# A fused attention, gated MLP and expert-routing kernel: a hand-written order for its first part, and one PSUM operand in the VectorE instructions of the routing

## The chip, the cores and the metric

The kernel is one launch on one core of a Trainium2 chip. The metric is the device time of that launch in microseconds (us), the median of several runs. Engines are named as in the profile: PE (TensorE), DVE (VectorE), ACT (ScalarE), POOL (GpSimd), and SP, whose queue issues nearly all the DMAs.

## What is computed

Three layers follow one another. B, H, S, DH are 8, 8, 576, 64; N is 4608 tokens, D 512, F 1024, E 8 experts, 576 tokens for each.

```python
scores = q @ k.T / 8 * Dmat              # Dmat[i,j] = gamma_h ** (i-j) for i >= j, else 0
x = (scores @ v)                         # heads side by side: [4608, 512]
y = ((x @ w1) * (x @ w2)) @ w3 @ w_out   # weights in float64, [512,1024] [1024,1024] [1024,512]
logits = y @ w_gate                      # [4608, 8]
# greedy: all logits in falling order; a token takes its expert if it has none yet
# and the expert has fewer than 576 tokens
out[token] = relu(y[token] @ ew1[e]) @ ew2[e]
```

## The kernel before

**Attention** goes by 36 tiles of 128 tokens (two chunks of 64). The decay is split into a factor on q and one on k: `att_scale` (L257, DVE for the first ten tiles), `att_T` transposes both on PE and copies them out on ACT, `att_QK`, `att_mask` (DVE), `att_P` (the k-v product of each chunk), `att_state` (DVE adds it to the running state), `att_AV`, and `att_out`: a copy by ACT, an add on DVE, then the result as a high part (ACT) and a low part (POOL, L345). Three tiles make one block of 384 tokens in `XT`.

**MLP.** `ab(i)` (L534) works a block: for each of 8 slices `f` it makes `x @ w1` and then `x @ w2`. Each of these is one **pass**: 12 matmuls of 128x384 (L549), three for each of 4 row blocks, since x and the weights are split into a high and a low part. After the first pass of a slice ACT copies the PSUM bank out (L556), after the second DVE multiplies (L558). The weights come as 64-bit floats in pieces of 256 columns (`load_pair`, 1 MB each); `conv` (L184) makes one unit of 128 columns from them with an absolute value on ACT (L196), four DVE instructions (L197 to L202), a copy on ACT (L215) and one more DVE instruction (L216). `ab(0)` needs all 16 units of w1 and w2; `LEAD` says how far ahead of a slice they are converted. w3 is multiplied by w_out beforehand (`w34_all`), whose first PE instructions are the transposes of L391.

**Order.** The generators above are interleaved by `merge` (L66), which takes from a side generator whatever the main one's declared cost pays for. That gives priorities; a list scheduler then orders each engine's instructions by its own estimate of when they are ready. In `begin` (L1093) attention tiles, conversions and `ab(0)`, `ab(1)` are merged so. `ORDER` (L23) is the order of the first loads on SP's queue: q, k, v of tiles 0 to 2, pieces w0 to w3 of the weights, three pieces c of the constants.

**Routing** (`route`, L787) finds one threshold per expert in five rounds. `propose` (L691) masks the logits that fail, takes the best expert of each token (`best`, L666) and moves the result to experts' rows (`LP`). `search` (L706) then takes 6 steps: two counts on DVE (L716, L717) and one on ACT (L719), a matmul that adds them up over partitions (L676), and three to four very short DVE instructions (L726, L728, L729, L725) that move the thresholds. `place` (L746) turns the result into the list of row numbers by comparisons with a ramp `iota` on DVE (L774) beside products on POOL (L773), and 48 matmuls (L779). All along, `merge` interleaves the 24 late output tiles (`y_late`, L875): each has 24 matmuls (L893), a high part by ACT (L888) and a low part by POOL (L889, 128x1024).

The eight experts follow (`expert`, L997), in a block whose order comes from the scheduler.

## Time and profile before

| | |
|---|---|
| median of 3 runs | 1333.74 us (1332.22 to 1334.24) |
| the profiled execution's own time | 1332.78 us |
| its span, first to last instruction | 1330.8 us |
| mean granted PE clock | 0.976 of full |
| PE busy | 1261.4 us (95%) |
| DVE busy | 573.7 us (43%) |
| ACT busy | 460.2 us (35%) |
| POOL busy | 262.7 us (20%) |

PE is busy nearly throughout, so the table says little by itself. Idle time of PE stands in three places: the first 140 us, the routing from about 710 to 886 us, and the end. The other engines matter where PE waits for them.

### The profile page before, as it was taken

The page shows a single profiled execution, that of the slowest core. Times are in us where ns is not written, and L with a number is a line of the kernel's source. Part 1 is how long each engine was busy: PE and PEld are TensorE (multiplying, and loading weights), DVE is VectorE, ACT ScalarE, POOL GpSimd, SP SyncE. Part 2 cuts the span into 40 slices and gives each one's busy share as a digit, 9 for nine tenths or more (in the row PEclk, how much of TensorE's full clock was granted, in tenths as well). Part 3 has the DMA queues.
Part 4 walks back from the last instruction along what each step waited for, and adds up shares of the span by engine and source line. Part 5 has one row for each costly group of instructions (what it writes and reads, how often), then busy time and mean ns, then how long its engine had stood idle before and what let it go on. Part 6 is the DMA issues. An engine that isn't in the chain of part 4 may idle for free. (4 is left out here: it accounts for less than half of the span.)

```text
span 1330.8 us, 27168 instructions
## 1 busy us (share of the span) xinstructions
PE 1261.4 (95%) x11406; PEld 1114.0 (84%) x11406; DVE 573.7 (43%) x1298; ACT 460.2 (35%) x987; POOL 262.7 (20%) x238
## 2 busy tenths in 40 slices
PE   5789999999999999999999899869999999999996
PEld 4688988889898998988997676669989989899885
DVE  6796544443232222212215777564524435335220
ACT  4443333343223222222222434234534435335321
POOL 0101111112112020211013533261211202201011
PEclk7799999999999999999999999879999999999999
DMA  8756444422313122242014112044524425334110
GB/s 229 231 168 183 128 136 137 118 75 55 81 23 87 35 66 77 68 127 81 10 48 163 52 40 87 34 155 135 170 69 138 146 84 159 113 118 151 40 45 28
DMA packets 156382, 136.00 MB, mean 102 GB/s; under 512 B 119264, under 2 KB 119520, under 8 KB 155232
## 3 DMA queue, kind: packets, MB, share of 16 engines
q1 hardware_dynamic: 150368, 115.35, 29.4%
q0 software_dynamic: 5888, 18.88, 4.3%
q8 instruction: 91, 1.49, 0.4%
q14 instruction: 35, 0.29, 0.1%
HBM read 107.19 MB, written 27.00 MB: 101 GB/s over the span
## 5 line engine op out<-in xcount | busy, mean ns | idle before, releaser
L549 PE MATMUL p<-x,ws 128*128 128x384 f32 x2304 | 424.1, 339 | 3.1 <-issue 1.6
L549 PEld LDWEIGHTS p<-x,ws 128*128 128x128 f32 x2304 | 398.2, 189 | 11.2 <-issue 4.7
L1032 PE MATMUL p<-ws,g 128*128 128x512 f32 x864 | 218.1, 394 | 1.9 <-DVE rs L1042 1.4
L1032 PEld LDWEIGHTS p<-ws,g 128*128 128x128 f32 x864 | 156.5, 188 | 31.5 <-DVE rs L1042 1.8
L893 PE MATMUL p<-ws,x 128*128 128x512 f32 x576 | 145.5, 406 | 0.0
L558 DVE TENSOR_TENSOR g<-p,ms 128x384 f32<-128x384 f32 x88 | 49.0, 557 | 182.1 <-PE p L549 179.2
L893 PEld LDWEIGHTS p<-ws,x 128*128 128x128 f32 x576 | 107.3, 193 | 20.5
L930 DVE TENSOR_TENSOR ws<-x,ws 128x512 fp32r<-128x512 f32 x120 | 80.7, 690 | 90.6 <-ACT ws L929 82.7
L261 POOL TENSOR_TENSOR a<-a,cst 128x512 f32<-128x512 f32 x52 | 54.6, 1051 | 304.6 <-DMA a<-q 232.3
L345 POOL TENSOR_TENSOR x<-a,x 128x256 fp32r<-128x256 f32 x64 | 49.3, 780 | 257.8 <-ACT x L344 257.8
L929 ACT ACTIVATE ws<-x 128x512 fp32r<-128x512 f32 x128 | 78.1, 628 | 63.4 <-DMA x<-ew 48.4
L556 ACT ACTIVATE ms<-p 128x384 f32<-128x384 f32 x96 | 47.0, 490 | 151.6 <-PE p L549 149.7
L1043 POOL DMA_INDIRECT out<-rs,idx x40 | 40.2, 1006 | 265.4 <-ACT g L1019 146.6
L601 PE MATMUL p<-ws,g 128*128 128x512 f32 x288 | 71.9, 398 | 0.0
L601 PEld LDWEIGHTS p<-ws,g 128*128 128x128 f32 x288 | 52.5, 188 | 13.3 <-issue 2.5
L1010 PE MATMUL p<-a,ws 128*128 128x320 f32 (+1 forms) x384 | 58.9, 303 | 0.5 <-issue 0.5
L1019 ACT ACTIVATE g<-py 128x256 fp32r<-128x256 f32 x96 | 31.5, 328 | 77.9 <-PE py L1010 68.1
L1010 PE MATMUL py<-a,ws 128*128 128x320 f32 (+1 forms) x384 | 57.5, 298 | 0.0
L1010 PEld LDWEIGHTS p<-a,ws 128*128 128x128 f32 x384 | 55.5, 195 | 2.0 <-issue 0.7
L1010 PE MATMUL p<-x,ws 128*128 128x320 f32 (+1 forms) x384 | 56.8, 297 | 0.0
L1010 PEld LDWEIGHTS py<-a,ws 128*128 128x128 f32 x384 | 55.1, 192 | 1.9
L1010 PE MATMUL py<-x,ws 128*128 128x320 f32 (+1 forms) x384 | 56.4, 296 | 0.3 <-DVE g L1020 0.3
(187 smaller groups left out, 1532.7 us busy)
## 6 DMA issues: line engine op xcount, KB each, us to landing
x<-ew SPq DMA_DIRECT2D x128, 256.0 KB, 2.9
y_scratch<-ms SPq DMA_DIRECT2D x36, 256.0 KB, 2.0
a<-k SPq DMA_DIRECT2D x64, 128.0 KB, 3.7
ws<-w SPq DMA_DIRECT2D x8, 1024.0 KB, 10.2
a<-q SPq DMA_DIRECT2D x62, 128.0 KB, 2.9
a<-v SPq DMA_DIRECT2D x31, 256.0 KB, 4.6
g_scratch<-g SPq DMA_DIRECT2D x8, 768.0 KB, 5.5
g<-g_scratch SPq DMA_DIRECT2D x4, 1536.0 KB, 6.7
```

The costliest lines, as they stand in the source:

```text
L261: (V if t < Q0 else G).tensor_tensor(xx, xx, tb_[:, :, None].to_broadcast([128, H, DH]), op=OP.mult)
L345: G.tensor_tensor(xl.rearrange("p (s a) i -> p s a i", s=2), f, xh.bitcast(F32).rearrange("p (s a) i -> p s a i", s=2), op=OP.subtract)
L549: PE.matmul(p[:, :TB], w[:, kk, fs], x[:, kk, :], start=(kk == 0 and j == 0), stop=(kk == 3 and j == 2))
L556: A.activation(a, p[:, :TB], AF.Copy)
L558: V.tensor_tensor(g[:, f, :], p[:, :TB], a, op=OP.mult)
L601: PE.matmul(p, x[:, f, ts], w[:, f, :], start=(f == 0 and j == 0), stop=(f == 7 and j == 2))
L893: PE.matmul(p, x[:, f, :], w[:, f, :], start=(f == 0 and j == 0), stop=(f == 7 and j == 2))
L929: A.activation(h, st, AF.Copy)
L930: low.tensor_tensor(lo[:, 512 * u:512 * u + 512], st, h.bitcast(F32), op=OP.subtract)
L1010: PE.matmul(p[:, :n], w[:, kk, fs], x[kk][:, ts], start=(kk == 0 and j == 0), stop=(kk == 3 and j == 2))
L1032: PE.matmul(p, x, w[:, f, :], start=(f == 0 and j == 0), stop=(f == 7 and j == len(ops) - 1))
L1043: st = G.indirect_dma_start(out=out, out_offset=bass.IndirectOffsetOnAxis(ap=idx[:n, 5 * e + o:5 * e + o + 1], axis=0), in_=ob[:n], in_off ...
```

## The change

Two separate edits. The first replaces the merges of `begin` by an order written out by hand, which PE, DVE and ACT keep as written (`manual_schedule`): `att_three` lists the steps of three attention tiles, `conv` yields after nearly every instruction, so that the merges can cut it, and the abs of the next unit (`conv_abs`) may be issued within the current one from the fourth unit on. One unit is now converted ahead in the first two slices (`LEAD`), the piece w1 of the weights moves behind tile 2's loads, and w2 and w3 are issued behind the k and v loads of tile 3. Slices 0 to 3 of `ab(1)` are mixed into the rest of `ab(0)` one step by one. Odd tiles up to 5 write their masked scores to a second buffer. The second edit puts four tensors of the routing into PSUM banks that attention has left: the search's step table `hs_`, the ramp `iota`, a copy of the logits `LBp`, and the masked logits `r1p`; and the update of `tau` becomes a `tensor_scalar`.

```diff
-LEAD = (3, 4, 4, 4, 4, 4, 4, 4)
+LEAD = (1, 1, 2, 2, 2, 2, 2, 2)
...
-ORDER = "q0 c0 k0 v0 c1 q1 k1 w0 v1 w1 q2 k2 v2 w2 w3 c2"
+ORDER = "q0 c0 k0 v0 c1 q1 k1 w0 v1 q2 k2 v2 w1 c2"
...
-    def conv(u):
+    begun = {}
+
+    def conv_abs(u):
         raw = raws.pop(u)
...
+        begun[u] = lo, hi, ta, tb, out
+
+    def conv(u, after=None):
+        if u not in begun:
+            conv_abs(u)
+        lo, hi, ta, tb, out = begun.pop(u)
         V.tensor_scalar(ta, ta, HIGH, LOW, op0=OP.min, op1=OP.max)
+        yield 350
         V.tensor_scalar(ta.bitcast(I32), ta.bitcast(I32), 3, 0x3FFFFFF8,
                         op0=OP.logical_shift_left, op1=OP.bitwise_and)
+        if after in raws and u[0] != "w3" and after[0] != "w3":
+            conv_abs(after)
+        yield 350
         V.scalar_tensor_tensor(tb.bitcast(I32), hi, -1073741824, ta.bitcast(I32),
                                op0=OP.bitwise_and, op1=OP.bitwise_or)
+        yield 600
         V.scalar_tensor_tensor(ta.bitcast(I32), lo, 29, tb.bitcast(I32),
                                op0=OP.logical_shift_right, op1=OP.bitwise_or)
...
         A.activation(hd, fl, AF.Copy)
+        yield 600
         V.tensor_tensor(ld, fl, hd.bitcast(F32), op=OP.subtract)
+        yield 600
...
+    AM2 = [RS[:, 512 + 256 * i:768 + 256 * i] for i in range(2)]
+
+    def masked(t):
+        return AM2 if t < 6 and t % 2 else AM
...
+    def next_q(t):
+        if t != 2:
+            att_load(t + (3 if t < 2 else 2), (0,))
+
+    def next_kv(t):
+        att_load(t + 3, (1,))
+        if t != 2:
+            att_load(t + (3 if t < 2 else 2), (2,))
+
+    def att_three(t):
+
+        att_scale(t)
+        yield 1200
+        att_T(t)
+        next_q(t)
+        att_scale(t + 1)
+        yield 1200
+        att_P(t)
+        att_QK(t)
+        att_T(t + 1)
+        next_q(t + 1)
+        yield 500
+        att_state(t)
+        att_mask(t)
+        yield 1300
+        att_P(t + 1)
+        att_QK(t + 1)
+        att_AV(t)
+        yield 300
+        att_mask(t + 1)
+        att_state(t + 1)
+        yield 1300
+        att_out(t)
+        next_kv(t)
+        yield 700
+        att_scale(t + 2)
+        yield 1200
+        att_T(t + 2)
+        next_q(t + 2)
+        yield 300
+        att_P(t + 2)
+        att_QK(t + 2)
+        att_AV(t + 1)
+        yield 300
+        att_mask(t + 2)
+        att_state(t + 2)
+        yield 1300
+        att_out(t + 1)
+        next_kv(t + 1)
+        yield 700
+        att_AV(t + 2)
+        yield 300
+        att_out(t + 2)
+        next_kv(t + 2)
+        yield 700
+
...
-    units = [(n, i, 0) for i in range(8) for n in ("w1", "w2")] + [("wo", i, 0) for i in range(8)]
+    units = [("w1", 0, 0), ("w1", 1, 0), ("w2", 0, 0), ("w2", 1, 0)]
+    units += [(n, i, 0) for i in range(2, 8) for n in ("w1", "w2")] + [("wo", i, 0) for i in range(8)]
...
         n = 2 * ((upto - 1) // 4) + 2 if upto <= 16 else upto - 8
+        n = 3 if upto == 7 else n
...
-        conv(units[i])
         nconv[0] += 1
+        yield from conv(units[i], units[i + 1] if 2 < i < 23 else None)
...
-                        conv_next()
+                        yield from conv_next()
...
-                    a = at_[nxt("a", 2)]
+                    a = at_[nxt("a", 2) if i > 1 else i]
...
-                yield 1960
+                yield 300 if i == 0 and f < 4 else 1960
...
-    hs_ = A2[:, 1056:1056 + 6 * TRIPS]
+    hs_, iota = PYb[0][:, 0:6 * TRIPS], PYb[0][:PT, 128:256]
+    LBp, r1p = PYb[1][:PT, 0:384], PX[1][:PT, 0:384]
...
-        V.scalar_tensor_tensor(r1, r1, NEG, LBf, op0=OP.mult, op1=OP.add)
-        best(r1)
-        V.tensor_tensor(f4(r2), f4(r1), bcast_j(r3), op=OP.is_lt)
-        V.scalar_tensor_tensor(r1, r2, NEG, r1, op0=OP.mult, op1=OP.add)
+        V.scalar_tensor_tensor(r1p, r1, NEG, LBp, op0=OP.mult, op1=OP.add)
+        best(r1p)
+        V.tensor_tensor(f4(r2), f4(r1p), bcast_j(r3), op=OP.is_lt)
+        V.scalar_tensor_tensor(r1, r2, NEG, r1p, op0=OP.mult, op1=OP.add)
...
-            V.scalar_tensor_tensor(tau, step[:, 0:1], hits, tau, op0=OP.mult, op1=OP.add)
+            V.tensor_scalar(tau, step[:, 0:1], hits, tau, op0=OP.mult, op1=OP.add)
...
-        V.tensor_tensor(o1, C("iota")[:PT, None, :40].to_broadcast([PT, 48, 40]),
+        V.tensor_tensor(o1, iota[:, None, :40].to_broadcast([PT, 48, 40]),
...
-            V.tensor_tensor(lo[:, a:b], C("iota")[:PT, None, :].to_broadcast([PT, 12, 128]),
+            V.tensor_tensor(lo[:, a:b], iota[:, None, :].to_broadcast([PT, 12, 128]),
...
     def route():
+        A.activation(LBp, LBf, AF.Copy)
+        A.activation(iota, C("iota")[:PT], AF.Copy)
         for a, steps in ROUNDS:
...
-    att = attention()
+    att = attention(6)
...
+    FINE = 35
 
     def begin():
-        merge(take(6), conv_some(LEAD[0]), RAT[0])
         a0, a1 = ab(0), ab(1)
-        s = take(2 * PER)
-        merge(take_from(a0, 8), s, RAT[1])
-        drain(s)
-        merge(turns(2, a0, take_from(a1, 8)), take(1), RAT[2])
+        with tc.manual_schedule(engines={PE.engine, V.engine, A.engine}):
+            c, s = conv_some(16), att_three(0)
+            drain(take_from(s, 7))
+            for n in range(2):
+                with tc.issue_after(loads[3, 1 + n].ins):
+                    load_more(8 if n else 7)
+            drain(take_from(c, 5))
+            drain(take_from(s, 3))
+            drain(take_from(c, 5))
+            drain(s)
+            s = att_three(3)
+            merge(take_from(a0, 8 + FINE), s, RAT[1])
+            drain(s)
+            drain(mix(a0, take_from(a1, 8), 0.44))
         w = w34_all()
-        merge(mix(a1, take(2 * PER - 1), 0.8), w, W34RATE)
+        merge(mix(a1, take(2 * PER), 0.8), w, W34RATE)
         for i in range(2, EARLY):
             merge(mix(ab(i), take(2 * PER), RAT[3]), w, W34RATE)
         drain(w)
```

Three places where the instructions move. The first is ACT's queue at the first pass of `ab(0)`. L556 (L628 now) is the copy of a pass's PSUM bank, L196 (L198) the abs of a conversion, L215 (L228) its high part, L276 (L297) the copy of transposes, L337 and L344 (L358, L365) the output of an attention tile; ws4 and ws5 hold raw weights, ws0 and ws2 the high parts of w1 and w2. Before:

```order
L215 ACTIVATE ws0_1_64<-g2_16_79 128x4x128
L276 ACTIVATE a1_10_73<-p0_82 128x8x64
L276 ACTIVATE a1_10_73<-p1_83 128x8x64
L215 ACTIVATE ws2_3_66<-g2_16_79 128x4x128
L337 ACTIVATE a1_10_73<-py_88 128x512
L344 ACTIVATE x0_7_70<-a1_10_73 128x4x64
L556 ACTIVATE ms_12_75<-p4_86 128x384
L196 ACTIVATE g2_16_79<-ws4_5_68 128x512 x2
```

Now:

```order
L365 ACTIVATE x0_7_70<-a1_10_73 128x4x64 x2
L628 ACTIVATE ms_12_75<-p4_86 128x384
L198 ACTIVATE g2_16_79<-ws4_5_68 128x512
L228 ACTIVATE ws2_3_66<-g2_16_79 128x4x128
L297 ACTIVATE a1_10_73<-p0_82 128x8x64
L297 ACTIVATE a1_10_73<-p1_83 128x8x64
L628 ACTIVATE ms_12_75<-p4_86 128x384
L198 ACTIVATE g2_16_79<-ws4_5_68 128x512
L198 ACTIVATE g2_16_79<-ws5_6_69 128x512
```

The abs of the first w2 unit stands behind the copy of the first pass, and that of the second behind the copy of the third pass; before, several units had been converted when the first pass ended.

The second place is DVE's queue from its first conversion on. L197, L198, L200, L202, L216 (L205, L207, L212, L215, L230) are the five instructions of a unit, L261 (L282) scales an attention tile, L288 (L309) masks, L312 (L333) adds to the state, L343 and L350 (L364, L371) make the output. Before:

```order
L197 TENSOR_SCALAR g2_16_79<-g2_16_79 128x512
L288 TENSOR_TENSOR a1_10_73<-py_88,cst_63 128x256
L198 TENSOR_SCALAR g2_16_79<-g2_16_79 128x512
L200 SCALAR_TENSOR_TENSOR ws4_5_68<-ws4_5_68,g2_16_79 128x4x128
L202 SCALAR_TENSOR_TENSOR g2_16_79<-ws4_5_68 128x512
L350 TENSOR_TENSOR x0_7_70<-p2_84,x0_7_70 128x4x64
L343 TENSOR_TENSOR a1_10_73<-p3_85,a1_10_73 128x2x128
L216 TENSOR_TENSOR ws1_2_65<-g2_16_79,ws0_1_64 128x4x128
L312 TENSOR_TENSOR a2_11_74<-p2_84,a2_11_74 128x256
```

Now:

```order
L371 TENSOR_TENSOR x0_7_70<-p2_84,x0_7_70 128x4x64
L364 TENSOR_TENSOR a1_10_73<-p3_85,a1_10_73 128x2x128
L205 TENSOR_SCALAR g2_16_79<-g2_16_79 128x512
L207 TENSOR_SCALAR g2_16_79<-g2_16_79 128x512
L212 SCALAR_TENSOR_TENSOR ws4_5_68<-ws4_5_68,g2_16_79 128x4x128
L215 SCALAR_TENSOR_TENSOR g2_16_79<-ws4_5_68 128x512
L230 TENSOR_TENSOR ws1_2_65<-g2_16_79,ws0_1_64 128x4x128
L282 TENSOR_TENSOR g0_14_77<-g0_14_77,cst_63 128x512
L282 TENSOR_TENSOR a2_11_74<-a2_11_74,cst_63 128x512
```

The output of tile 0 now stands ahead of the first conversion, each conversion runs through, and tile 2 is scaled only behind it.

The third place is DVE's queue in the routing, at one proposal and the first search step. py and p2, p3 are PSUM, a2 and rs SBUF, LB the logits. Before:

```order
L696 TENSOR_TENSOR a2_11_74<-LB_81,p0_82 96x384
L697 SCALAR_TENSOR_TENSOR a2_11_74<-a2_11_74,LB_81 96x384
L668 TENSOR_REDUCE rs_13_76<-a2_11_74 96x48
L699 TENSOR_TENSOR a2_11_74<-a2_11_74,rs_13_76 96x384
L700 SCALAR_TENSOR_TENSOR a2_11_74<-a2_11_74 96x384
L716 TENSOR_SCALAR rs_13_76,rh_98<-a2_11_74,rs_13_76 128x288
L726 SCALAR_TENSOR_TENSOR rs_13_76<-p0_82,cst_63 128x3
L728 SCALAR_TENSOR_TENSOR rs_13_76<-a2_11_74,rs_13_76 128x3
L729 SCALAR_TENSOR_TENSOR rs_13_76<-a2_11_74,rs_13_76 128x1
```

Now:

```order
L769 TENSOR_TENSOR a2_11_74<-LB_81,p0_82 96x384
L770 SCALAR_TENSOR_TENSOR p3_85<-a2_11_74,py_88 96x384
L741 TENSOR_REDUCE rs_13_76<-p3_85 96x48
L772 TENSOR_TENSOR a2_11_74<-p3_85,rs_13_76 96x384
L773 SCALAR_TENSOR_TENSOR a2_11_74<-a2_11_74,p3_85 96x384
L789 TENSOR_SCALAR rs_13_76,rh_98<-a2_11_74,rs_13_76 128x288
L799 SCALAR_TENSOR_TENSOR rs_13_76<-p0_82,cst_63 128x3
L801 SCALAR_TENSOR_TENSOR rs_13_76<-py_88,rs_13_76 128x3
L802 TENSOR_SCALAR rs_13_76<-py_88,rs_13_76 128x1
```

The instructions are the same ones in the same order; those that read two SBUF tensors now read one from SBUF and one from PSUM.

## Rows read from the trace of the kernel before

**Rows 1.** Stretches by span time: length, busy PE, PEld, DVE, ACT, POOL; clock, DMA, GB/s

```profile
...
0.00:20.00 20.00, 9.37 (x224) 7.74 (x224) 8.76 (x21) 6.83 (x13) 1.16 (x7) 0.94 0.84 221
20.00:40.00 20.00, 10.36 (x202) 8.79 (x204) 19.86 (x40) 8.72 (x16) 2.08 (x3) 0.50 0.80 210
40.00:60.00 20.00, 18.26 (x248) 16.15 (x249) 13.14 (x30) 8.68 (x19) 2.71 (x4) 0.71 0.81 267
60.00:80.00 20.00, 17.27 (x310) 15.34 (x310) 19.96 (x41) 12.07 (x24) 2.23 (x2) 1.00 0.58 162
...
500.00:600.00 100.00, 100.00 (x1109) 88.43 (x1112) 20.47 (x46) 23.93 (x49) 14.43 (x16) 1.00 0.31 91
```

**Rows 2.** Waits of PE, 0 to 142 us: waiter, releaser, us, times, longest

```profile
PE p L274 <- DVE a L261: 15.5, 6, 5.5
```

**Rows 3.** Groups of instructions on PE, 0 to 140.8 us: busy us, mean ns | idle before

```profile
L549 PE MATMUL p<-x,ws 128*128 128x384 f32 x372 | 70.2, 345 | 3.1 <-issue 1.6 <-POOL x L345 1.3
```

**Rows 4.** Groups on DVE, 0 to 47.5 us: busy us, mean ns | idle before

```profile
L261 DVE TENSOR_TENSOR a<-a,cst 128x512 f32<-128x512 f32 x11 | 7.6, 689 | 7.0 <-DMA cst<-cst 3.9 <-DMA a<-q 2.0 <-DMA a<-k 1.1
...
L216 DVE TENSOR_TENSOR ws<-g,ws 128x512 fp32r<-128x512 f32 x8 | 5.5, 687 | 0.0
...
L343 DVE TENSOR_TENSOR a<-p,a 128x256 f32<-128x256 f32 x5 | 1.9, 421 | 0.0
```

**Rows 5.** Timeline of the first part: start us, us, engine, instruction [idle before <-releaser]

```profile
15.73 0.69 PE L300 MATMUL p<-a 64*64 64x64 f32 x32 [1.67 <-DMA a<-v]
...
20.50 2.08 PE L329 MATMUL p<-a,a 64*64 64x64 f32 x32
...
47.52 6.65 PE L549 MATMUL p<-x,ws 128*128 128x384 f32 x24
...
52.27 0.49 ACT L556 ACTIVATE ms<-p 128x384 f32<-128x384 f32 x1 [4.32 <-PE p L549]
...
55.77 6.51 PE L549 MATMUL p<-x,ws 128*128 128x384 f32 x36
...
140.86 1.03 PE L391 MATMUL p<-cst,g 128*128 128x128 f32 x8
```

**Rows 6.** Groups on ACT, 0 to 60 us

```profile
L196 ACT ACTIVATE g<-ws 128x512 f32<-128x512 f32 x12 | 7.5, 666 | 3.4 <-DMA ws<-w 3.4
L276 ACT ACTIVATE a<-p 128x512 f32<-128x512 f32 x10 | 5.6, 592 | 11.5 <-PE p L274 11.4
```

**Rows 7.** Groups on DVE in the routing, 709 to 882 us

```profile
L728 DVE SCALAR_TENSOR_TENSOR rs<-a,rs 128x3 f32<-128x3 f32 x25 | 27.0, 1081 | 2.7
...
L774 DVE TENSOR_TENSOR g<-cst,rs 96x1536 f16<-96x1536 f32 x4 | 11.4, 2894 | 0.0
...
L697 DVE SCALAR_TENSOR_TENSOR a<-a,LB 96x384 f32<-96x384 f32 x6 | 5.1, 851 | 0.2
...
L726 DVE SCALAR_TENSOR_TENSOR rs<-p,cst 128x3 f32<-128x3 f32 x30 | 4.9, 163 | 21.7 <-PE p L676 21.7
L696 DVE TENSOR_TENSOR a<-LB,p 96x384 f32<-96x384 f32 x6 | 3.3, 545 | 1.3 <-PE p L694 1.3
```

**Rows 8.** Waits of PE in the routing, 709 to 890 us

```profile
PE p L676 <- DVE rs L717: 11.9, 12, 2.2
...
PE p L779 <- POOL ws L773: 2.6, 2, 2.0
PE p L673 <- DVE a L700: 1.7, 3, 0.7
```

**Rows 9.** Timeline in the search: two steps' late matmuls, a held DVE instruction and POOL's

```profile
726.87 3.54 PE L893 MATMUL p<-ws,x 128*128 128x512 f32 x9
...
731.10 2.75 PE L893 MATMUL p<-ws,x 128*128 128x512 f32 x11
...
839.45 2.40 POOL L889 TENSOR_TENSOR x<-a,x 128x1024 fp32r<-128x1024 f32 x1 [4.33 <-ACT x L888]
839.47 2.40 DVE L728 SCALAR_TENSOR_TENSOR rs<-a,rs 128x3 f32<-128x3 f32 x1
```

More of the change, by code (lines that the diff above doesn't have):

```diff
@@ L236, in build @@
     loaded = set()
+    loads = {}
     def att_load(t, which=(0, 1, 2), eng=SP):
@@ L248, in att_load @@
                 if i == 2:
-                    eng.dma_start(x[p:p + n].rearrange("p (h d) -> p h d", h=H),
+                    loads[t, i] = eng.dma_start(x[p:p + n].rearrange("p (h d) -> p h d", h=H),
                                  src[b, :, s:s + n, :].rearrange("h s d -> s h d"))
@@ L252, in att_load @@
                     for r in range(2):
-                        eng.dma_start(x[p:p + n].rearrange("p (c r d) -> p r c d", c=4, r=2)[:, r],
+                        loads[t, i] = eng.dma_start(x[p:p + n].rearrange("p (c r d) -> p r c d", c=4, r=2)[:, r],
                                      src[b, 4 * r:4 * r + 4, s:s + n, :].rearrange("h s d -> s h d"))
@@ L287, in att_mask @@
         for s in range(2):
-            V.tensor_tensor(AM[s].rearrange("p (c i) -> p c i", c=4),
+            V.tensor_tensor(masked(t)[s].rearrange("p (c i) -> p c i", c=4),
                             PYb[s][:, 0:256].rearrange("p (c i) -> p c i", c=4),
@@ L330, in att_AV @@
                               buf(t)[2][halves(u), 256 * s + 64 * c:256 * s + 64 * c + 64],
-                              AM[s][halves(u), 64 * c:64 * c + 64], start=True, stop=True, skip_group_check=True)
+                              masked(t)[s][halves(u), 64 * c:64 * c + 64], start=True, stop=True, skip_group_check=True)
     def att_out(t):
@@ L350, in att_out, with attention @@
                 V.tensor_tensor(xl, po, xh.bitcast(F32), op=OP.subtract)
-    def attention():
+    def next_q(t):
[50 more added lines that the diff above has]
+        yield 700
+    def attention(first):
         def T(t):
@@ L356, in T @@
                 att_T(t)
-                if t != 2:
-                    att_load(t + (3 if t < 2 else 2), (0,))
-        T(0)
-        T(1)
-        att_P(0)
-        att_QK(0)
-        att_mask(0)
-        att_state(0)
+                next_q(t)
+        T(first)
+        T(first + 1)
+        att_P(first)
+        att_QK(first)
+        att_mask(first)
+        att_state(first)
         yield 2500
-        for t in range(NT):
+        for t in range(first, NT):
             att_AV(t)
@@ L376, in attention @@
             T(t + 2)
-            att_load(t + 3, (1,))
-            if t != 2:
-                att_load(t + (3 if t < 2 else 2), (2,))
+            next_kv(t)
             yield 1400
@@ L458, in conv_next @@
         i = nconv[0]
-        if i >= len(units):
-            return False
-        conv(units[i])
         nconv[0] += 1
+        yield from conv(units[i], units[i + 1] if 2 < i < 23 else None)
         if i == 3:
@@ L468, in conv_next @@
             load_more(i + 4)
-        return True
     def conv_some(n):
         for _ in range(n):
-            conv_next()
-            yield 2500
+            yield from conv_next()
     def w34_all():
         while nconv[0] < 25:
-            conv_next()
+            drain(conv_next())
             yield 2600
@@ L485, in w34_all @@
                 if u < 16:
-                    conv_next()
+                    drain(conv_next())
                     hl.append(w34_T(*divmod(u, 2)))
@@ L544, in ab @@
                     while nconv[0] < min(need, 16):
-                        conv_next()
+                        yield from conv_next()
                 p = mm_bank()
@@ L1079, in mix @@
             yield from side
-    def turns(n, *gens):
-        gens = list(gens)
-        while gens:
-            for g in gens[:]:
-                for _ in range(n):
-                    c = next(g, None)
-                    if c is None:
-                        gens.remove(g)
-                        break
-                    yield c
+    FINE = 35
     def begin():
-        merge(take(6), conv_some(LEAD[0]), RAT[0])
         a0, a1 = ab(0), ab(1)
-        s = take(2 * PER)
-        merge(take_from(a0, 8), s, RAT[1])
-        drain(s)
-        merge(turns(2, a0, take_from(a1, 8)), take(1), RAT[2])
+        with tc.manual_schedule(engines={PE.engine, V.engine, A.engine}):
[12 more added lines that the diff above has]
+            drain(mix(a0, take_from(a1, 8), 0.44))
         w = w34_all()
-        merge(mix(a1, take(2 * PER - 1), 0.8), w, W34RATE)
+        merge(mix(a1, take(2 * PER), 0.8), w, W34RATE)
         for i in range(2, EARLY):
```

## The prediction

> **What bounds the kernel now.** I read the stretches first. From 500 to 600 us PE is busy for 100.00 of 100 us at a granted clock of 1.00 [rows 1]; where it is full like that, a saving upstream is carried on to the end and nothing on another engine counts. It is not full in two places that the change touches. In the first 60 us it works 9.37, 10.36 and 18.26 of each 20 us, and the clock falls to 0.50 in the second stretch, where DVE has 19.86 of 20 [rows 1]. The waits of PE say why: the transposes of L274 wait 15.5 us in six pieces for the scaling on DVE, L261 [rows 2], which stands among conversions there. So DVE, and PE's clock behind it, bound the start. The second place is the routing. Its waits are L676 on DVE's counts, 11.9 us in 12 pieces, L673 on DVE's masking, 1.7, and L779, 2.6 in two, put down to POOL [rows 8].
>
> The profiled execution took 1332.78 us, 0.96 less than the median 1333.74. I make the sum against 1332.8 and add 0.96 at the end. A difference under 0.2%, 2.7 us, is what I call no change.
>
> **The routing, step by step.** L728 works on 3 elements per partition and means 1081 ns, 25 times; L726, also 3 elements but with its first operand in PSUM, means 163 [rows 7]. L697 and L696 both work on 96x384: with two SBUF operands 851, with one of them in PSUM 545 [rows 7]. The timeline shows the stretching: an L728 starts at 839.47 and takes 2.40 us, and POOL's low part L889 starts at 839.45 and takes 2.40 [rows 9]. Both end together. A DVE instruction with two SBUF tensors is held as long as POOL's runs; one with a PSUM operand is not. The change gives each held kind a PSUM operand: `hs_` (L728), `r1p` and `LBp` (L697, L668, L699, L700), `iota` (L774).
>
> DVE's loss is 25 x (1.08 - 0.16) = 23 us in L728 alone, but PE mostly works beside it: late output matmuls fill a search step, 11 of them in 2.75 us [rows 9]. So I price what PE waits, not what DVE loses:
> - L676: 11.9 us [rows 8]. With L728 near 0.2 us, the counts start up to 2.2 us earlier in just the steps that lost. All 11.9 go.
> - L673: 1.7 [rows 8], behind L697 to L700, goes too.
> - The clock. After such waits nine late matmuls take 3.54 us, and soon after eleven take 2.75 [rows 9]: 0.393 against 0.250 each, so 9 x 0.143 = 1.3. Without the waits the clock has no cause to fall: 1.3.
> - `place`: L774 means 2894 ns for 1536 elements [rows 7]. At L696's rate per element it would be 545 x 4 = 2.2; part of L696's 545 is paid once per instruction, so I estimate 1.75. Four save 4.6 on DVE, but PE also has its late matmuls there, and what it can get back is L779's 2.6; I take 2.2, since POOL's own product L773 stays.
>
> Together 11.9 + 1.7 + 1.3 + 2.2 = 17.1. The first search step now has 10 late matmuls beside it instead of 12 or more, so less cover; I leave 0.6 for that and take **-16.5**. The two added ACT copies stand at the start of the routing, where ACT has no work that PE waits for: nothing, or 1.0 if that cover is gone, by two ACT copies of 0.49 [rows 5]. `tau` as `tensor_scalar` has the same three operands and is one element wide: nothing. Ends: -18 (another 0.9 of clock, nothing left over), and -11 (ACT's count L719 ends just behind DVE's, so that only half of L676's 11.9 goes).
>
> [...]
>
> **The first part, step by step.** Before, the first pass of `ab(0)` starts at 47.52 [rows 5], by when eight units have been converted [rows 4]. Now only two need be. PE's start is the same up to the load of v: L300 waits for it to 15.73 [rows 5]. P, QK and AV of the first two tiles, at the low clock like the L329 group that takes 2.08 [rows 5], make about 5 us: 20.7, or 18.7 if v comes 2 us sooner because w1 no longer loads beside it. Then the written order leaves one long chain: output of tile 0, two units, scaling, transposes and their copies for tile 2, mask, state, output of tiles 1 and 2. I count some 30 instructions on DVE, ACT and POOL one behind the other, with 0.42 to 0.69 on DVE [rows 4] and 0.59 to 0.67 on ACT [rows 6]; at 0.62 that is an estimated 18.6. The first pass starts near **39**.
>
> Eight us are not won, though. After the first pass, ACT's queue has the copy of the pass ahead of the abs of the w2 unit that the second pass needs. That copy waits for the pass's last matmul (before, L556 waited 4.32 for PE [rows 5]). So PE then waits for copy 0.49 [rows 5], abs 0.67 [rows 6] and the rest of a conversion, four DVE instructions and ACT's high part one behind the other, about 2.5: 3.65 in all. A pass costs 36 matmuls in 6.51, so 12 in 2.17, at full clock, and twice that, 4.3, at 0.50; 24 took 6.65, half and half [rows 5]. So: 39 + 4.4 (first pass, low clock) + 3.65 + 6.5 (two passes, half and half) + 4.25 (again a w2 unit behind the third pass's copy; a transpose's copy stands ahead of it) = 57.8. Before, the first 36 matmuls were done at 55.77 + 2.17 = 57.9 [rows 5]. Level.
>
> From there both have 372 - 36 = 336 pass matmuls left before the first transposes of w3 at 140.86 [rows 3, 5], 336 x 0.181 = 60.8, and nearly the same attention. DVE was full from 60 to 80 as well, 19.96 of 20 [rows 1], and must still convert the same units, now closer to their use. I take **0** for the first part. Ends: -8 (the first passes at full clock 4.4, v early 2, part of the 2.7 idle of 60 to 80 [rows 1]), and +8 (two more w2 units exposed, 2 x 3.65, or the copies late again). The moved DMAs: w2 and w3 are issued behind tile 3's k and v near 21 us; 2 MB at this stretch's 210 GB/s [rows 1] are 10 us; the third pair of units wants them past 50, so they are hidden; if not, each late piece adds a few us. Tile 3's own loads stand ahead of them on SP.
>
> **Sum**: 1332.8 - 16.5 + 0 = 1316.3, and 0.96: **1317**.
>
> **Rivals.**
> 1. *The written order feeds PE densely.* If ACT's copies and conversions lie under the passes and the clock stays at 1.00 after 39, the three passes end at 39 + 6.5 + 3.65 = 49, some 9 earlier than 57.9: 1308. For it: only two units stand ahead of the pass, and the 15.5 of L274 [rows 2] vanish. Against it: the abs behind the copy. Chance 0.26.
> 2. *The routing gives about half.* Another wait takes L676's place, or the PSUM operand costs time of its own: with a tenth of L696's 545 [rows 7] on each of 114 instructions, 6 us, all on the path. 16.5 becomes 9 to 10: 1324. For it: in steps of 2.75 us, DVE's chain and PE's cover are close. Chance 0.10. [...]
> 3. *The change doesn't free DVE*: POOL still holds instructions with one SBUF operand. 1334, give or take 6. Against it: L726 and L696 [rows 7]. Chance 0.07.
> 4. *Slower: the clock stays at its low level through the first eight passes,* because PE stops behind each copy of a pass. Passes 2 and 3 then cost 2.2 more, five further passes 2.2 each, and two more w2 units stay exposed, 7.3: 2.2 + 11 + 7.3 = 20.5 over the forecast, 1337.5. It decides once the first part loses over 19 us. For it: 0.50 from 20 to 40 [rows 1], with PE about half busy. Against it: from 60 to 80, PE works 17.27 of 20 us and is granted 1.00. Chance 0.06.
>
> My forecast has 0.51. Its own ends are 1334 - 18 - 8 = 1308 and 1334 - 11 + 8 = 1331 if all goes one way; both together are unlikely, so 1310 to 1326. Taking in most of rivals 1 and 2, with the routing's -18 on top of the first part's -9 and some clock, the range is **1303 to 1328**; outside lie rivals 3 and 4 and the tails, under 0.2. Rivals 1, 2 and the forecast give faster 0.87; half of rival 3's spread is faster by over 2.7 or nearly, so 0.89; no change 0.04; slower 0.07.
>
> **What would show it.** In the changed kernel's trace: L728's successor L801 near 0.22 us beside POOL's low parts, L774's near 1.75, L676's wait gone to about 0, the clock at 1.00 around 727. The first pass starting near 39, a PE idle of 3 to 4 us behind it that ends on a conversion, the third pass ending near 58, the w3 transposes near 141. I am wrong on the start if those come 8 us sooner or later, and on the routing if DVE's instructions still end with POOL's, or if L676 waits over 5 us for another engine.

## The result: slower by 0.8%, and the two edits pull in opposite directions

| | before | changed |
|---|---|---|
| median | 1333.42 us (1332.22 to 1334.24, 4 runs) | 1343.49 us (1341.28 to 1345.93, 4 runs) |
| ratio to before | | 1.0077 (95% interval 1.0057 to 1.0096) |
| profiled execution, own time and span | 1332.78, 1330.8 | 1341.28, 1339.3 |
| mean granted PE clock | 0.976 | 0.972 |
| first late output matmul (L893, now L968) starts | 709.7 | 739.6 |
| the matmuls of `place` that close the routing (L779, now L852) start | 875.6 | 886.6 |

The forecast was 1317, in a range of 1303 to 1328. The last two lines of the table show where it failed: the first part brings the kernel to its late matmuls 29.9 us later, the routing gives back 18.9 of it, and 2.3 more come back up to the experts' first product (L1010, which starts at 889.12; L1085 in the changed kernel, at 897.88).

**The first part.** The changed kernel's stretches, same columns as [rows 1]:

```profile
0.00:20.00 20.00, 7.86 (x208) 7.03 (x208) 6.11 (x15) 4.50 (x8) 0.66 (x6) 0.85 0.88 224
20.00:40.00 20.00, 6.98 (x209) 6.25 (x209) 10.99 (x25) 6.55 (x13) 2.53 (x4) 0.59 0.86 223
40.00:60.00 20.00, 13.59 (x132) 12.12 (x132) 7.99 (x14) 4.29 (x8) 1.72 (x2) 0.71 0.41 131
60.00:80.00 20.00, 14.22 (x150) 11.60 (x150) 13.84 (x29) 7.01 (x14) 0.12 (x1) 0.74 0.55 155
```

DVE, which had 19.86 and 19.96 of 20 us in two of these stretches [rows 1], now has 10.99 and 13.84 there, and ACT has 6.55 and 7.01 instead of 8.72 and 12.07: none of the three is full, and each waits for another. PE's waits up to the first transposes of w3 (waiter, releaser, us, times, longest; compare [rows 2]):

```profile
PE p L295 <- DVE g L282: 8.9, 1, 8.9
PE p L621 <- ACT ws L228: 7.7, 4, 3.5
PE p L295 <- DVE a L282: 6.6, 2, 5.6
PE p L321 <- DMA a<-v: 4.1, 1, 4.1
PE p L621 <- ACT ms L628: 2.5, 2, 2.3
```

The first line is one single wait: the transposes of tile 2 for its scaling, which stands behind a whole conversion in DVE's queue. With the third line it makes 15.5 us, as much as the six waits before [rows 2], so in sum PE waits no longer for the scaling than it did. The second line is new: passes that wait for the high part of a unit of weights. The timeline shows one such stop:

```profile
39.91 0.69 PE L621 MATMUL p<-x,ws 128*128 128x384 f32 x1 [2.30 <-ACT x L365]
...
45.39 0.49 ACT L628 ACTIVATE ms<-p 128x384 f32<-128x384 f32 x1 [5.53 <-PE p L621]
...
45.78 0.65 ACT L198 ACTIVATE g<-ws 128x512 f32<-128x512 f32 x1
...
48.84 0.63 ACT L228 ACTIVATE ws<-g 128x512 fp32r<-128x512 f32 x1 [2.41 <-DVE g L215]
...
49.52 7.04 PE L621 MATMUL p<-x,ws 128*128 128x384 f32 x24 [3.52 <-ACT ws L228]
...
56.64 0.49 ACT L628 ACTIVATE ms<-p 128x384 f32<-128x384 f32 x1 [6.20 <-PE p L621]
...
57.03 1.27 ACT L198 ACTIVATE g<-ws 128x512 f32<-128x512 f32 x2
...
60.80 1.42 PE L621 MATMUL p<-x,ws 128*128 128x384 f32 x4 [2.51 <-ACT ws L228]
```

The first pass starts at 39.91, close to the forecast (39). The copy of its bank (45.39) has been waiting for 5.53 us; only behind it comes the abs of the next unit (45.78), then four DVE instructions, then the high part (48.84), and only then the second pass (49.52). The third pass ends at 49.52 + 7.04 = 56.56. Then the same stop comes once more (56.64, 57.03), and the fourth pass starts at 60.80. With these two, 6.0 of the 7.7 us that the passes wait for L228 are over; what the forecast put at nothing is what comes behind, where other waits follow and the matmuls stay slow. One row for the stretch from the end of the third pass to the first transposes of w3, of the kernel before:

```profile
57.90:140.86 82.96, 75.41 (x1027) 71.28 (x1026) 65.87 (x136) 38.16 (x75) 13.27 (x15) 1.00 0.62 176
```

and of the changed kernel:

```profile
56.56:161.60 105.04, 89.85 (x1088) 81.38 (x1088) 84.82 (x166) 44.39 (x86) 9.05 (x11) 0.90 0.49 141
```

The stage takes 105.04 instead of 82.96 us. It holds 61 matmuls more, since the changed kernel had done fewer by the end of its third pass (472 of all kinds, against 660 before). PE is idle for 15.2 us in it instead of 7.6, and its matmuls are slower: granted clock 0.90 instead of 1.00. Of the idle time and the clock, the group of the 372 pass matmuls shows both (changed kernel, 0 to 162 us; compare [rows 3]):

```profile
L621 PE MATMUL p<-x,ws 128*128 128x384 f32 x372 | 80.8, 376 | 16.7 <-ACT ws L228 7.7 <-ACT ms L628 2.5 <-ACT x L365 2.3
```

80.8 us busy instead of 70.2 for the same 372 matmuls, and 16.7 of idle time in front of them instead of 3.1. From there to the late matmuls the changed kernel takes 578.00 us instead of 568.84. Not all of these 9 us are a loss, since it has 128 more matmuls there: it had done that many fewer ahead of the transposes of w3.

Up to the first late matmul both kernels have done the same 8117 matmuls. One row each, before and changed:

```profile
0.00:709.70 709.70, 679.77 (x8117) 612.37 (x8118) 278.22 (x581) 227.32 (x454) 108.21 (x124) 0.98 0.37 102
```

```profile
0.00:739.60 739.60, 690.07 (x8117) 619.38 (x8117) 285.84 (x581) 226.61 (x454) 109.55 (x124) 0.96 0.35 97
```

So of the 29.9 us, 19.6 are idle time of PE (49.53 instead of 29.93) and 10.3 are slower matmuls (690.07 instead of 679.77 us busy). I go by the time that the same matmuls take, because the clock column alone can mislead: e_begin below has the same first part, and from 40 to 60 us the column says 1.00 there and 0.71 in the changed kernel, at nearly the same busy time (13.92 and 13.59 us).

**The routing.** DVE's groups in the changed kernel, 738 to 895 us (compare [rows 7]):

```profile
L847 DVE TENSOR_TENSOR g<-py,rs 96x1536 f16<-96x1536 f32 x4 | 6.7, 1744 | 0.0
L801 DVE SCALAR_TENSOR_TENSOR rs<-py,rs 128x3 f32<-128x3 f32 x25 | 5.5, 221 | 2.7
...
L770 DVE SCALAR_TENSOR_TENSOR p<-a,py 96x384 f32<-96x384 f32 x6 | 3.3, 557 | 0.3
L741 DVE TENSOR_REDUCE rs<-p 96x48 f32<-96x384 f32 x6 | 3.3, 553 | 0.2
```

L801, L728 before, means 221 ns instead of 1081; L847 means 1744 instead of 2894. None of the moved instructions is held by POOL any more: the longest L801 takes 223 ns, L798 219, L770 559, L772 553, L773 549, L847 1745. One place in the timeline shows it:

```profile
753.86 2.41 POOL L964 TENSOR_TENSOR x<-g,x 128x1024 fp32r<-128x1024 f32 x1
...
754.60 2.79 PE L968 MATMUL p<-ws,x 128*128 128x512 f32 x11
...
755.06 0.22 DVE L801 SCALAR_TENSOR_TENSOR rs<-py,rs 128x3 f32<-128x3 f32 x1
```

Here L801 starts and ends inside POOL's low part. PE's wait for the counts, 11.9 us before [rows 8], is gone; this is all that is left in the search:

```profile
PE p L749 <- ACT ms L792: 0.4, 1, 0.4
```

The routing from its first late matmul to `place`'s matmuls, of the kernel before and then of the changed one:

```profile
709.70:875.60 165.90, 148.33 (x652) 111.87 (x652) 119.21 (x333) 59.49 (x120) 71.18 (x34) 0.97 0.21 78
```

```profile
739.60:886.60 147.00, 142.62 (x651) 111.02 (x651) 79.74 (x334) 60.48 (x122) 67.05 (x35) 0.99 0.24 88
```

18.9 us less: PE idles 4.4 instead of 17.6 (13.2), and nearly the same matmuls (651 and 652) take 142.6 instead of 148.3 (5.7, at a granted clock of 0.99 instead of 0.97). DVE is busy 39.5 us less.

### The profile page after: what moved, and what is told of

The parts are those of the page before. It is cut to its first block, busy times and chain, and to the rows that moved or that the text cites. A ratio compares the mean times of both kernels' runs of the same rounds, so it can differ in the third digit from the quotient of the medians.

```text
span 1339.3 us, 27178 instructions
## 1 busy us (share of the span) xinstructions
PE 1264.9 (94%) x11406; PEld 1119.1 (84%) x11406; DVE 537.7 (40%) x1298; ACT 459.5 (34%) x989; POOL 255.5 (19%) x238
## 5 line engine op out<-in xcount | busy, mean ns | idle before, releaser
L621 PE MATMUL p<-x,ws 128*128 128x384 f32 x2304 | 435.0, 344 | 17.3 <-ACT ws L228 7.7
L621 PEld LDWEIGHTS p<-x,ws 128*128 128x128 f32 x2304 | 405.9, 192 | 28.4 <-ACT ws L228 8.9
L968 PE MATMUL p<-ws,x 128*128 128x512 f32 x576 | 142.0, 401 | 0.0
L968 PEld LDWEIGHTS p<-ws,x 128*128 128x128 f32 x576 | 105.9, 191 | 20.7 <-issue 0.4
L282 POOL TENSOR_TENSOR a<-a,cst 128x512 f32<-128x512 f32 x52 | 56.1, 1079 | 327.0 <-DMA a<-q 167.9
L628 ACT ACTIVATE ms<-p 128x384 f32<-128x384 f32 x96 | 47.0, 489 | 154.4 <-PE p L621 154.4
L1085 PE MATMUL p<-a,ws 128*128 128x320 f32 (+1 forms) x384 | 58.7, 301 | 0.5 <-ACT a L1068 0.5
L1085 PE MATMUL p<-x,ws 128*128 128x320 f32 (+1 forms) x384 | 57.3, 298 | 0.6 <-DVE g L1095 0.6
L1085 PE MATMUL py<-a,ws 128*128 128x320 f32 (+1 forms) x384 | 57.2, 297 | 0.0
L1085 PEld LDWEIGHTS p<-a,ws 128*128 128x128 f32 x384 | 55.1, 193 | 2.0 <-ACT a L1068 0.7
L1085 PE MATMUL py<-x,ws 128*128 128x320 f32 (+1 forms) x384 | 56.4, 296 | 0.3 <-DVE g L1095 0.3
L1085 PEld LDWEIGHTS py<-a,ws 128*128 128x128 f32 x384 | 54.8, 191 | 1.9
```

Source lines behind the costliest of these rows:

```text
L282: (V if t < Q0 else G).tensor_tensor(xx, xx, tb_[:, :, None].to_broadcast([128, H, DH]), op=OP.mult)
L621: PE.matmul(p[:, :TB], w[:, kk, fs], x[:, kk, :], start=(kk == 0 and j == 0), stop=(kk == 3 and j == 2))
L628: A.activation(a, p[:, :TB], AF.Copy)
L968: PE.matmul(p, x[:, f, :], w[:, f, :], start=(f == 0 and j == 0), stop=(f == 7 and j == 2))
L1085: PE.matmul(p[:, :n], w[:, kk, fs], x[kk][:, ts], start=(kk == 0 and j == 0), stop=(kk == 3 and j == 2))
```

## The experiments

All were timed against runs of the kernel before on the same chip. The rows come from four chips, on which the kernel before takes 1331.80 to 1333.87 us, so rows are best compared by their ratios. "Fixed" means that an engine keeps the written order in `begin`.

| run | what it is | median us | ratio to before (95%) |
|---|---|---|---|
| e_route | before, new routing | 1310.05 | 0.9834 (0.9815 to 0.9854) |
| e_begin | change, old routing | 1361.75 | 1.0225 (1.0198 to 1.0252) |
| e_lead | change, old numbers of units ahead | 1333.59 | 1.0013 (1.0002 to 1.0024) |
| e_free | change, nothing fixed | 1307.04 | 0.9816 (0.9794 to 0.9839) |
| e_pe | change, PE alone fixed | 1317.12 | 0.9896 (0.9871 to 0.9920) |
| e_dve | change, DVE alone fixed | 1322.98 | 0.9932 (0.9912 to 0.9952) |
| e_act | change, ACT alone fixed | 1321.89 | 0.9927 (0.9911 to 0.9944) |
| e_da | change, DVE and ACT fixed | 1334.48 | 1.0016 (1.0003 to 1.0030) |
| e_abs | change, abs always a unit ahead | 1333.32 | 0.9999 (0.9984 to 1.0013) |
| w_scale | change, tiles 2 and 5 scaled sooner | 1339.21 | 1.0044 (1.0030 to 1.0058) |
| w_both | e_abs and w_scale | 1330.95 | 0.9987 (0.9975 to 1.0000) |
| f_lead2 | e_free, one unit more ahead | 1309.97 | 0.9821 (0.9799 to 0.9844) |
| f_lead4 | e_free, old numbers of units ahead | 1315.87 | 0.9862 (0.9835 to 0.9888) |
| f_abs | e_free with the edit of e_abs | 1307.31 | 0.9813 (0.9791 to 0.9836) |
| f_scale | e_free with the edit of w_scale | 1309.48 | 0.9828 (0.9806 to 0.9850) |
| e_search | before, search's table in PSUM only | 1316.20 | 0.9887 (0.9870 to 0.9903) |

### Each edit alone: e_route and e_begin

e_route is the kernel before with the routing hunks of the diff; e_begin is the changed kernel without them.

> The kernel before with the routing's part of the change alone. If the two edits are independent and the first part alone loses, this is 1333.4 less what the routing took between the first late matmul and the place matmuls (165.6 us before, 146.8 in the changed kernel): 1313 to 1316. If the shorter routing in the changed kernel owes something to the shifted start, it is 1320 or more.

> The change with the routing's operands as before, so the written order alone. Independent edits: 1343.5 + 18 to 21 = 1361 to 1365. If the edits work on each other: below 1355.

The routing alone gives 22 us (a ratio of 0.9834), somewhat more than the 1313 to 1316 us that I expected and than the 18.9 + 2.3 read from the two traces; the first part alone loses 30, as expected. Both together make +8, and the change measured +10: the edits are independent within what the runs can tell. The routing part is right, and larger than I forecast (16.5); the question is the first part.

### Too few units ahead, or the written order itself: e_lead and e_free

Two theories. The number of units converted ahead fell from 3 or 4 to 1 or 2; or the fixed order is at fault, whatever the numbers. e_lead:

```diff
-LEAD = (1, 1, 2, 2, 2, 2, 2, 2)
+LEAD = (3, 4, 4, 4, 4, 4, 4, 4)
...
             drain(take_from(s, 3))
-            drain(take_from(c, 5))
+            drain(take_from(c, 15))
             drain(s)
```

> The change with four units converted ahead of the first pass and the old numbers of units ahead (3, then 4) instead of 1 and 2; the order is still written. Theory 1, too few units ahead, so that DVE and ACT stand idle between passes and PE waits for each unit: the first pass starts later, near 46, the waits for L228 and L230 behind it go, and the time is 1318 to 1326. Theory 2, the written order itself (ready work queued behind waiting work on DVE and ACT): not more than 5 us better than the change, 1338 to 1344.

e_free takes the fixing away and leaves the program's order as it is written:

```diff
-        with tc.manual_schedule(engines={PE.engine, V.engine, A.engine}):
+        if True:
```

> The change without the fixed order: the same program order and the same units ahead, but the scheduler may reorder PE, DVE and ACT in the first part. Theory 1 (units ahead): some gain, since abs and conversions of the next unit can move ahead of a pass's copy only as far as the program asks for them; 1330 to 1340. Theory 2 (the order itself): 1312 to 1322, like the routing's part alone.

e_free is at 1307.04, 36 us under the change, and the fastest so far. Its program asks for the same work in the same sequence, with as few units ahead. e_lead wins 10 of the 36, more than "not more than 5", and far from 1318 to 1326; so the first theory falls as the main cause, and the fixed order is it. The order of the loads, the units ahead and the sequence of the program are the same in e_free, so none of these by itself makes the loss. e_free's stretches:

```profile
20.00:40.00 20.00, 14.74 (x241) 13.20 (x242) 15.81 (x30) 8.99 (x18) 4.91 (x5) 0.57 1.05 243
40.00:60.00 20.00, 19.69 (x300) 17.00 (x302) 19.34 (x41) 11.25 (x22) 2.42 (x2) 1.00 0.78 235
60.00:80.00 20.00, 17.35 (x246) 15.39 (x237) 19.62 (x41) 11.40 (x22) 2.70 (x3) 1.00 0.81 242
```

DVE is full again from 40 us on, and the clock is 1.00. Its timeline at the first pass shows what the scheduler does differently:

```profile
32.17 1.01 PE L621 MATMUL p<-x,ws 128*128 128x384 f32 x2 [1.86 <-ACT x L365]
...
37.66 0.49 ACT L628 ACTIVATE ms<-p 128x384 f32<-128x384 f32 x1 [5.54 <-PE p L621]
37.94 4.28 PE L621 MATMUL p<-x,ws 128*128 128x384 f32 x23
38.04 0.62 ACT L228 ACTIVATE ws<-g 128x512 fp32r<-128x512 f32 x1
```

The pass starts at 32.17, and at its end PE goes on without a wait (37.94). ACT's copy has waited here as well, 5.54 us, but what stands behind it (38.04) is the high part of a later unit; the one that the second pass needs was finished before. The third pass ends at 42.22; by then e_free has done 472 matmuls, as many as the changed kernel at 56.56, and converted four units. The stretch from there to the transposes of w3 holds the same 1088 matmuls as in the changed kernel:

```profile
42.22:127.20 84.98, 80.51 (x1088) 74.14 (x1089) 78.66 (x161) 43.05 (x82) 8.82 (x9) 1.00 0.70 209
```

84.98 us instead of 105.04, of which PE is idle for 4.5 instead of 15.2. The first late matmul starts at 704.5.

### Which engine's queue: e_pe, e_dve, e_act, e_da

The same line of `begin` again, with one or two engines left in `engines={...}`.

> The change with the written order kept by PE alone; DVE and ACT may be reordered. With nothing fixed it was 1307, with all three fixed 1343.5. Theory D (DVE's queue: the scaling of tile 2 stands behind a whole conversion, and conversions behind scaling and multiplications that wait for PE): 1305 to 1315. Theory P (PE's queue: passes that are ready stand behind attention matmuls that wait for DVE or ACT, and the other way round): 1328 or more.

> The change with the written order kept by DVE alone. Theory D: 1328 to 1343. Theory P, or a theory A that ACT's queue (abs and high parts behind the copy of a pass) makes the loss: 1305 to 1318.

> The change with the written order kept by ACT alone. Theory A (the abs of the next unit and the high part stand behind the copy of a pass, which waits for PE): 1328 to 1343. Theories D and P: 1305 to 1318. If none of the three single engines gives 10 us or more, the loss needs two of them fixed together.

None of the three theories that I had named is enough: each run lies outside both of its ranges. PE's fixed queue costs 10 us over e_free, DVE's 16, ACT's 15; all three together 36 (by the ratios 11, 15, 15 and 35). In PE's waits up to 200 us, these lines have grown most over e_free; they cover only a part of each loss. DVE fixed: tile 2's scaling behind a conversion, as in the change (1.6 in e_free).

```profile
PE p L295 <- DVE g L282: 6.4, 1, 6.4
```

ACT fixed: the passes wait for the high part of a unit (no such wait in e_free).

```profile
PE p L621 <- ACT ws L228: 4.4, 3, 2.8
```

PE fixed: neither of these. Passes start late twice without a releaser that the profile shows ("issue"), and one waits longer for the output of a tile (1.9 in e_free).

```profile
PE p L621 <- issue: 5.5, 2, 3.4
PE p L621 <- ACT x L365: 4.3, 1, 4.3
```

> The written order kept by DVE and ACT, PE free. If the losses are separate: 1307 + 16 + 15 = 1338. If one queue's wait hides in the other's (ACT's abs waits for a copy, DVE for that abs): 1323 to 1328. Either way PE free can't undo more than its own 10 us: if all the loss hung on PE's order, 1307 to 1315.

1334.48: 27 over e_free, between the two cases. That is 4 less than 16 + 15, so these two losses overlap a little; PE's order makes up the rest of the 36.

Since each of these runs has 8117 or 8118 matmuls up to its first late one, the traces split what is lost there into idle time of PE and slower matmuls:

| run | first late matmul at | PE idle before it | PE busy before it |
|---|---|---|---|
| before | 709.7 | 29.9 | 679.8 |
| e_free | 704.5 | 23.7 | 680.8 |
| e_pe | 715.8 | 32.8 | 683.0 |
| e_dve | 721.0 | 36.3 | 684.7 |
| e_act | 718.5 | 31.3 | 687.2 |
| e_da | 731.5 | 42.7 | 688.8 |
| change | 739.6 | 49.5 | 690.1 |
| e_abs | 732.9 | 41.6 | 691.4 |
| e_lead | 732.9 | 49.6 | 683.3 |

Traces with the same first part (before, e_route and e_search; the change and e_begin) differ by up to 4 us in the idle time and 1 us in the busy time. The fixed order's 35 us over e_free are 25.8 of idle time and 9.3 of slower matmuls. In e_lead the passes' waits for L228 are gone, as theory 1 said, but the idle time has stayed as long as in the change: PE waits elsewhere, for instance 20.3 us for the scaling instead of 15.5. What it gained are faster matmuls.

### Two places in the written order mended: e_abs, w_scale, w_both

e_abs issues the abs of the next unit within the unit before, from the first unit on:

```diff
-        yield from conv(units[i], units[i + 1] if 2 < i < 23 else None)
+        yield from conv(units[i], units[i + 1] if i < 23 else None)
```

> The change, all three engines in the written order, with the abs of the next unit issued within the unit before from the first unit on, not from the fourth. The prediction's own mechanism was that the abs of a w2 unit stands behind the copy of a pass. If that carries the loss of the written order: two to three stops of 3.5 us fall to 1.5 and the clock rises, 1328 to 1336. If it is only one of many such places: 1339 to 1343.

1333.32, 10 us better (6.4 between the two profiled executions): the larger of the two cases. The group of pass matmuls in e_abs, 0 to 162 us:

```profile
L621 PE MATMUL p<-x,ws 128*128 128x384 f32 x372 | 80.5, 375 | 9.7 <-ACT x L365 2.3 <-ACT ms L628 1.9 <-ACT ws L228 1.9
```

The idle time in front of the passes falls from 16.7 to 9.7, that for L228 from 7.7 to 1.9. Their busy time stays at 80.5: the clock hasn't come back, though that case counted on it. So this one place makes about a quarter of the loss.

w_scale moves `att_scale(t + 2)` ahead of `att_out(t)` in `att_three`, and the counts in `begin` with it:

```diff
+        att_scale(t + 2)
+        yield 1200
         att_out(t)
         next_kv(t)
         yield 700
-        att_scale(t + 2)
-        yield 1200
         att_T(t + 2)
```

> The change, all three engines in the written order, with tile 2 (and 5) scaled on DVE ahead of the output of tile 0 (and 3), so that its transposes don't wait for a whole conversion. In the changed kernel PE waits 8.9 us there. If that wait moves the end: 1333 to 1337. If the work behind it is only reached sooner to wait elsewhere (for the units): 1340 to 1344.

1339.21, 4 us better: between the two cases, and not decided by itself. With both:

> The change in the written order on all three engines, with both mended places: the abs of the next unit within the unit before from the first unit on, and tiles 2 and 5 scaled ahead of the output of tiles 0 and 3. If the two are separate waits: 1343.5 - 10 - 4 = 1329. If the second only moves the wait to the unit behind it, now earlier by the abs: 1333, as with the abs alone.

1330.95, again between 1329 and 1333. The trace shows where a good part of the scaling's 8.9 went: PE's wait for it falls to 1.6, and this stands at the head of the list instead:

```profile
PE py L304 <- ACT a L297: 7.0, 2, 5.6
```

The longer of the two waits in the timeline:

```profile
25.55 0.63 ACT L228 ACTIVATE ws<-g 128x512 fp32r<-128x512 f32 x1 [3.51 <-DVE g L215]
26.09 1.07 ACT L297 ACTIVATE a<-p 128x512 f32<-128x512 f32 x2
...
26.72 1.51 PE L304 MATMUL py<-a 64*64 64x64 f32 x29 [5.55 <-ACT a L297]
```

The transposes come sooner, and PE now waits for ACT's copy of them (26.09), which stands in ACT's fixed queue behind the high part of a unit (25.55); that in turn has waited for DVE. A hole in one queue moves into the next.

### Can the free order be bettered: f_lead2, f_lead4, f_abs, f_scale

The edits of e_lead (f_lead4), of half of it (f_lead2: `LEAD = (2, 2, 3, 3, 3, 3, 3, 3)`), of e_abs and of w_scale on top of e_free.

> No fixed order, with one unit more ahead (2, 2, then 3) than the change has. With the change's 1, 1, 2 and no fixed order it was 1307. If fewer units ahead are better because attention and the first passes come sooner: 1308 to 1312. If more cover for the passes is better: 1303 to 1306.

> No fixed order, with the numbers of units ahead of the kernel before (3, then 4) and four units converted first. If the small lead is what gains against the kernel before's start (which with the new routing gives 1310): 1309 to 1313. If the lead makes no difference once the order is free: 1305 to 1309.

> Nothing fixed, and the abs of the next unit issued within the unit before from the first unit on. If the loss by the abs is only a matter of a queue kept as written: no difference to 1307, 1305 to 1309. If the program's order weighs by itself: 1300 to 1304.

> Nothing fixed, with tiles 2 and 5 scaled ahead of the output of tiles 0 and 3. If the scheduler did this already: 1305 to 1309. If it didn't: 1301 to 1304.

f_abs is at 1307.31, no difference to e_free: the edit that is worth 10 us in fixed queues is worth nothing where the scheduler places the abs itself. f_scale and f_lead2 lie 2 to 3 us above e_free, inside the intervals. f_lead4 is at 1315.87, above both of its cases, 0.9862 against 0.9816, with intervals that just overlap: more units ahead do not help, if anything they cost. Against e_route (0.9834) e_free is not told apart by the intervals; it and f_abs are the fastest versions that I have, 25 and 26 us under the kernel before that ran beside them, and the new routing makes nearly all of that.

### What of the routing's gain is the search: e_search

Only `hs_` moved to PSUM and `tau` by `tensor_scalar`, on the kernel before.

> The kernel before with the step table hs_ in PSUM and the tau update as tensor_scalar, nothing else: the search's short instructions alone, 55 of the 114 with a PSUM operand outside of L725's. The routing's part as a whole gave 22 us. If PE's waits for the counts (11.9) and the clock that falls after them (5.7 in the whole part) are all due to the held short instructions: 1314 to 1317. If the proposals and the place step carry half: 1320 to 1324.

1316.20, 15.6 us of the 22. Its DVE groups in the routing:

```profile
L774 DVE TENSOR_TENSOR g<-cst,rs 96x1536 f16<-96x1536 f32 x4 | 11.4, 2896 | 0.0
L699 DVE TENSOR_TENSOR a<-a,rs 96x384 f32<-96x384 f32 x6 | 10.0, 1672 | 0.2
...
L728 DVE SCALAR_TENSOR_TENSOR rs<-py,rs 128x3 f32<-128x3 f32 x25 | 5.5, 222 | 2.7
...
L668 DVE TENSOR_REDUCE rs<-a 96x48 f32<-96x384 f32 x6 | 5.0, 827 | 0.2
```

and PE's wait behind the proposals:

```profile
PE p L673 <- DVE a L700: 2.6, 3, 1.6
```

L728 is free at 222 ns while L699 and L774, which still have two SBUF operands, are held as before or longer (1672 against 1467, 2896 against 2894). So the cause is the operand of the single instruction, not a POOL that has become lighter. I put the six us that are left down to the proposals and `place`, which I had priced at 1.7 and 2.2, and some clock; no run separates them.

## Why the prediction was wrong, step by step

- **L728 and its kin are freed by a PSUM operand**: right. 221 ns measured, 0.22 forecast; L774's successor 1.744, forecast 1.75; L676's wait from 11.9 to 0.4; none of them ends with POOL.
- **The routing's sum, -16.5**: right in its mechanism, too small in one term. The waits gave 13.2 against 11.9 + 1.7 = 13.6, `place` 2.3 against 2.2. The clock's term was 1.3 and measured 5.7: I priced one place, [rows 9], and left the other stops of PE unpriced. e_route's 22 agrees.
- **The first pass near 39**: right (39.91), and the stop of 3.5 us behind it stands where it was said to be. **The third near 58**: luck. The last term of the sum, 4.25, is the stop behind the third pass, so by the sum the third pass ends at 53.55 and the fourth starts at 57.8. Measured are 56.56 and 60.80, both 3 us later.
- **"From there both have 372 - 36 = 336 pass matmuls left", "and nearly the same attention", "I take 0"**: this is the step that failed. I took the state at 58 us as equal because the same number of pass matmuls was done, took DVE to be as full as before, and so put the waits and the clock behind that point at nothing. By then 472 matmuls of all kinds were done instead of 660, and three units converted instead of eight; DVE had 13.84 of 20 us from 60 to 80 instead of 19.96. The stretch to the transposes of w3 took 105.04 us instead of 82.96, and these started at 161.60, 20.7 us late, where I had called 8 a sign of being wrong. The fewer units are not the cause by themselves: e_free comes out of its third pass with 472 matmuls done and four units, and does the same 1088 matmuls in 84.98. So the term at nothing was what the fixed queues cost behind the third pass: 20.1 us against the free order, 10.7 of idle time and 9.3 of slower matmuls. Another 14.3 lie ahead of it (56.56 against 42.22); there the written order is within 3 us of the kernel before, as forecast, but not of what the same program does when free.
- **The range's upper end, +8 for two more exposed units**: the true loss was 30. Rival 4 came nearest, with PE stopping behind copies, the clock low (0.71 and 0.74 in 40 to 80 us) and 1337.5 as its time, though the abs behind the copy makes only 10 of the 36 us. I gave it 0.06, on the ground that the kernel before has 1.00 with 17.27 of 20 busy. The changed kernel's 14.22 of 20 is not that case.
- **Rival 1's ground that the 15.5 us of waits for the scaling vanish**: they didn't; they are 8.9 + 6.6 in the changed kernel.
- **The order rows** in the section on the change told that ACT's abs stands behind a copy. I read them at one place. The experiments show that all three queues have such places, worth 10, 16 and 15 us, and that mending the two that I could name gives 10 and 4.
- **Rival 2's PSUM operand that costs time of its own**, a tenth of L696's 545 ns on each of 114 instructions (24 in the proposals, 85 in the searches, 5 in `place`): the traces show this for one kind at most. The prediction's 851 against 545 ns doesn't tell, since the 851 holds what POOL adds: the shortest L697 takes 553, the shortest L770 557. By the shortest times no other kind of the 114 became longer by more than these 4 ns. L725 reads one row of `hs_`, from SBUF before and from PSUM now; its shortest, median and longest time before:

```profile
L725 DVE SCALAR_TENSOR_TENSOR rs<-cst,rs,a x25: 210/219/2042, 712.8 to 837.5; 128x3 f32<-128x3 f32 x25
```

and in the changed kernel:

```profile
L798 DVE SCALAR_TENSOR_TENSOR rs<-cst,rs,py x25: 207/214/219, 746.1 to 851.2; 128x3 f32<-128x3 f32 x25
```

5 ns less in the median, and the 2042 are gone. One kind did become longer, the update of `tau`, which I had put at nothing. Before and now:

```profile
L729 DVE SCALAR_TENSOR_TENSOR rs<-a,rs x30: 206/213/1320, 720.2 to 843.5; 128x1 f32<-128x1 f32 x30
```

```profile
L802 DVE TENSOR_SCALAR rs<-py,rs x30: 268/270/278, 749.9 to 855.6; 128x1 f32<-128x1 f32 x30
```

57 ns more in the median. Here the operation changed together with the operand, and no run tells which of the two it is.

What stays open is which stops come with slower matmuls. Idle time and slower matmuls don't go together one to one: e_abs has 8.0 us less idle time than the change at nearly the same busy time (1.3 us more), e_lead the same idle time and 6.7 us less busy time. No run here shows why.

## What to carry to other kernels

An order written by hand for engines that keep it strictly is a bet on the moment when every operand is ready: one instruction that waits for another engine holds the ready work behind it (here the copy that waited 5.53 us for PE held an abs), and the holes of three queues nearly add up (10, 16 and 15 us alone, 36 together). Here the same program was fastest where the scheduler placed the instructions; test such a fixing engine by engine before keeping it. And where an instruction on DVE stands beside POOL's work on SBUF, look for a free PSUM bank for one of its two operands: here the same instruction fell from a mean of 1081 ns to 221.

When two orders are called level at some moment, count all the work that is done by then, not one kind of it: 36 pass matmuls were done in both kernels, but 472 matmuls in all against 660. And ask what waits the rest of the order still holds.
